# First norm of an adaLN, linear attention and SwiGLU block: the shift term of tile 1 moves to GpSimd, and the transposes of tiles 1 to 3 are reordered around the scale columns

## The chip, the cores and the metric

The kernel runs on one core of a Trainium2 chip. The metric is the device time of one execution in microseconds (us); lower is better. The profile's span (first to last instruction) is about 1.8 us shorter than the device time: the profiled run of the kernel before has a span of 827.4 us and a time of 829.23 us. Every run also reports the mean granted clock of TensorE, as a share of full speed. Six of the profiles kept, those of the kernel before and of the changed kernel among them, hold no clock records; a clock of 1.000 there means only that no slower stretch was recorded.

## The reference, cut to what matters

```python
mod = silu(c) @ w_mod                      # six rows of 1024: sa, ca, ga, sb, cb, gb
h = layernorm(x) * (1 + ca) + sa           # x: 2048 x 1024, bf16
x = x + ga * linear_attention(h, wqkv, wo) # 32 heads of 32
h = layernorm(x) * (1 + cb) + sb
x = x + gb * ((silu(h @ w_gate) * (h @ w_up)) @ w_down)
```

The change touches the first `layernorm` and the column sums that make `1 + ca`, for the first 512 rows only (tiles 0 to 3 of 128 rows). They are what stands between the start of the program and the first matmul of the q projection.

## The kernel before

The parts that matter, with cuts marked `[...]`. A helper records every operation in program order for each engine and adds the semaphore waits. An engine runs its own operations in the order written. Reads and writes of PSUM are ordered by whole banks: an engine that reads any part of a bank waits for the last TensorE operation recorded on that bank.

```python
def mod_sc(w, c0, ms):            # one column of 128 sums for each m: 8 matmuls of one column
    for m in ms:
        for kt in range(NDT):
            P.pe("matmul", out=PS[:, 0, c0 + m:c0 + m + 1], lhsT=w[:, kt, m*128:(m+1)*128], rhs=SILUC[:, kt:kt+1], [...])

def tile_transposes(*js):         # column blocks dt and dt+1 of all four tiles share a PSUM bank
    for dt in range(NDT):
        for j in js:
            P.pe("transpose", out=PSB[:, 4 + dt // 2, [...]], in_=XRES[:, j, dt*128:(dt+1)*128], identity=IDENT[:])

def act_xn(st, mean):             # shift term on VectorE, normalization on ScalarE
    P.dve("tensor_scalar", out=NMR[:, st:st+1], in0=mean, scalar1=RSTD[:, st:st+1], scalar2=-1.0, op0=ALU.mult, op1=ALU.mult)
    P.act("activation", out=XRES[:, st, :], in_=XRES[:, st, :], func=ACT.Identity, scale=RSTD[:, st:st+1], bias=NMR[:, st:st+1])

def warm(n=1, bank=2):            # matmuls that only keep TensorE's clock up
    for _ in range(n):
        P.pe("matmul", out=PS[:, bank, :], lhsT=IDENT[:], rhs=E1[:, 0, :], start=True, stop=True)

warm(13, bank=3)
[...]
act_xn(0, MV[:, 0, 0:1])
tile_transposes(0)
warm(5, bank=3)
act_var(1)                        # variance of tile 1, on VectorE
s2_[2]()                          # statistics of tile 2
P.dve("tensor_scalar", out=VE[:, 2:3], in0=MV[:, 2, 1:2], scalar1=EPS, scalar2=None, op0=ALU.add)
P.pool("tensor_tensor", out=RSTD[:, 1:3], in0=VE[:, 1:3], in1=NEGHALF[:, 0:2], op=ALU.pow)
s3_[0](); s3_[1](); s3_[2]()      # statistics of tile 3
ln1_rstd1(3)
act_xn(1, SUMX[:, 1:2])
ln1_xn(2)                         # normalization of tile 2, on VectorE
tile_transposes(2)
mod_sc(WCA, 8, range(2))          # scale columns 0-255
ln1_xn(3)
fin_ca(0, 2)
tile_transposes(1, 3)
mod_sc(WCA, 8, range(2, 4))
h0_first(0, "dve")                # first operand of q: transposed block times scale, read from PSUM
[...]
```

## Time and profile before

| | before |
|---|---|
| time, first three runs | 832.71, 833.0, 830.86 us (median 832.71) |
| profiled run | 829.23 us, span 827.4 us, granted clock 1.000 |
| TensorE busy | 816.5 us, 99% of the span |

The page's busy line of the kernel before:

```profile
PE 816.5 (99%) x4244; PEld 376.4 (45%) x4323; DVE 311.3 (38%) x665; ACT 197.4 (24%) x336; POOL 39.8 (5%) x57
```

TensorE is the limit nearly everywhere. Note also 4244 matmul records beside 4323 weight loads: 79 matmul records are missing, so a gap between two matmuls of this trace may be a missing record. Weight-load records (PEld) are complete.

The timeline of the first norm of the kernel before. Columns: start us, us, engine, line, operation, out<-in, count, and in brackets the engine's idle time before it and what ended that.

```profile
8.20 0.62 PE L176 MATMUL ps<-ident,xres 128*128 128x128 bf16 x8 [0.18 <-ACT xres L176]
8.66 1.24 PE L176 MATMUL ps<-e,ident 128*128 128x512 bf16 x5
...
8.95 0.20 DVE L176 TENSOR_SCALAR nmr<-sumx,rstd 128x1 f32<-128x1 f32 x1
...
9.24 1.24 ACT L176 ACTIVATE xres<-xres,nmr,rstd 128x1024 bf16<-128x1024 bf16 x1 [1.10 <-DVE nmr L176]
...
9.74 0.61 PE L176 MATMUL ps<-ident,xres 128*128 128x128 bf16 x8
...
10.18 0.54 PE L176 MATMUL ps<-siluc,wca 128*128 128x1 bf16 x16
...
10.59 1.05 PE L176 MATMUL ps<-ident,xres 128*128 128x128 bf16 x16
...
11.09 0.88 DVE L176 TENSOR_SCALAR ht<-ps,modcol 128x512 bf16<-128x512 bf16 x2 [0.17 <-PE ps L176]
...
11.48 0.54 PE L176 MATMUL ps<-siluc,wca 128*128 128x1 bf16 x16
...
11.86 1.20 PEld L176 LDWEIGHTS ps<-ht,wqk 128*128 128x128 bf16 x7
```

Read it as one queue on TensorE: tile 0, warm-up, tile 2, columns, tiles 1 and 3, columns, q. Each group starts where the one before it stops issuing. The `us` of a group runs to the modelled end of its last matmul, so neighbours overlap. Tile 1 is normalized from 9.24 to 10.48, because its shift term (`nmr`) waits on VectorE behind tile 3's statistics; TensorE wants it at 10.59.

### The profile page before, as it was taken

The page shows a single profiled execution, that of the slowest core. Times are in us where ns is not written, and L with a number is a line of the kernel's source. Part 1 is how long each engine was busy: PE and PEld are TensorE (multiplying, and loading weights), DVE is VectorE, ACT ScalarE, POOL GpSimd, SP SyncE. Part 2 cuts the span into 40 slices and gives each one's busy share as a digit, 9 for nine tenths or more (in the row PEclk, how much of TensorE's full clock was granted, in tenths as well). Part 3 has the DMA queues.
Part 4 walks back from the last instruction along what each step waited for, and adds up shares of the span by engine and source line. Part 5 has one row for each costly group of instructions (what it writes and reads, how often), then busy time and mean ns, then how long its engine had stood idle before and what let it go on. Part 6 is the DMA issues. An engine that isn't in the chain of part 4 may idle for free.

```text
span 827.4 us, 10429 instructions
## 1 busy us (share of the span) xinstructions
PE 816.5 (99%) x4244; PEld 376.4 (45%) x4323; DVE 311.3 (38%) x665; ACT 197.4 (24%) x336; POOL 39.8 (5%) x57
## 2 busy tenths in 40 slices
PE   8999999999999999999999999999999999999998
PEld 4544444444444444444444444444444444444444
DVE  5797987476945521121221112122111211221111
ACT  4757643123241111011111101111110111111011
POOL 1010000000130000020000003000000300000000
DMA  9969656866397985600455570045557004553000
GB/s 320 298 146 230 151 156 158 180 191 254 75 256 235 290 255 153 173 26 24 131 152 151 154 177 25 20 131 153 152 153 182 26 19 128 152 151 85 0 26 26
DMA packets 199359, 119.31 MB, mean 144 GB/s; under 512 B 57992, under 2 KB 183056, under 8 KB 199312
## 3 DMA queue, kind: packets, MB, share of 16 engines
q1 hardware_dynamic: 199296, 118.65, 53.5%
q8 instruction: 34, 0.56, 0.3%
q14 instruction: 13, 0.11, 0.0%
q10 hardware_dynamic: 16, 0.00, 0.0%
HBM read 100.67 MB, written 4.33 MB: 127 GB/s over the span
## 4 chain that ended last, share of the span: by engine, by line
PE 96%; DVE 2%; issue 1%; DMA 0%; ACT 0%; DVEq 0%; ACTq 0%
PE ps L176 96%; DVE acc L176 1%; DMA xres<-in_A_x_dram 0%; DVE stats L176 0%; DVE pkt L176 0%; DVE e L176 0%; ACT xres L176 0%; DVE pqt L176 0%; ACT e L176 0%; DVE mv L176 0%; DVE xres L176 0%; DVE ht L176 0%; DVE ve L176 0%; DVE nmr L176 0%; DVEq L247 0%
## 5 line engine op out<-in xcount | busy, mean ns | idle before, releaser
L176 PE MATMUL ps<-h2t,gug 128*128 128x512 bf16 x878 | 210.1, 379 | 0.9
L176 PE MATMUL ps<-h2t,guu 128*128 128x512 bf16 x878 | 209.9, 379 | 0.9
L176 DVE TENSOR_TENSOR at<-sg,ps 128x512 bf16<-128x512 bf16 x112 | 77.1, 688 | 282.7 <-PE ps L176 270.5
L176 ACT ACTIVATE sg<-ps 128x512 bf16<-128x512 f32 x112 | 66.9, 597 | 309.7 <-PE ps L176 298.3
L176 PEld LDWEIGHTS ps<-h2t,guu 128*128 128x128 bf16 x896 | 87.7, 98 | 105.7
L176 PEld LDWEIGHTS ps<-h2t,gug 128*128 128x128 bf16 x896 | 87.6, 98 | 105.5
L176 PE MATMUL ps<-wd_a,at 128*128 128x512 bf16 (+1 forms) x502 | 111.9, 377 | 0.5
L176 PE MATMUL ps<-ht,wqk 128*128 128x512 bf16 x499 | 110.3, 379 | 0.8
L176 PE MATMUL ps<-wd_b,at 128*128 128x512 bf16 (+1 forms) x377 | 84.6, 377 | 0.4
L176 PEld LDWEIGHTS ps<-wd_a,at 128*128 128x128 bf16 x512 | 50.1, 98 | 59.7
L176 DVE TENSOR_TENSOR ut<-att,gb_b 128x512 bf16<-128x512 bf16 (+1 forms) x32 | 14.1, 442 | 167.0 <-ACT att L176 167.0
L176 PEld LDWEIGHTS ps<-ht,wqk 128*128 128x128 bf16 x512 | 49.5, 98 | 58.7 <-DVE ht L176 0.2
L176 ACT ACTIVATE att<-ps 128x512 bf16<-128x512 f32 (+1 forms) x32 | 17.4, 591 | 182.1 <-PE ps L176 182.1
L176 PEld LDWEIGHTS ps<-wd_b,at 128*128 128x128 bf16 x384 | 37.6, 98 | 44.7
L176 PE MATMUL ps<-mw,pqt 128*128 128x512 bf16 x249 | 55.6, 379 | 1.5 <-issue 1.2
L176 PE MATMUL ps<-pk,xres 128*128 128x512 bf16 x250 | 55.4, 379 | 0.6 <-issue 0.5
L176 POOL TENSOR_SCALAR h2t<-h2t,modcol 128x512 bf16<-128x512 bf16 x32 | 26.4, 842 | 383.3 <-DMA h2t<-xn 383.3
L176 ACT ACTIVATE e<-ps 128x512 bf16<-128x512 f32 x56 | 33.2, 604 | 31.7 <-PE ps L176 19.4
L176 PEld LDWEIGHTS ps<-mw,pqt 128*128 128x128 bf16 x256 | 24.7, 98 | 31.3 <-issue 1.8
L176 PEld LDWEIGHTS ps<-pk,xres 128*128 128x128 bf16 x256 | 24.7, 98 | 29.9 <-issue 0.9
L176 ACT ACTIVATE junk<-xres 128x1024 bf16<-128x1024 bf16 x24 | 25.4, 1058 | 35.6 <-DVE xres L176 35.3
L176 DVE SCALAR_TENSOR_TENSOR xres<-ps,xres 128x512 bf16<-128x512 f32 x32 | 21.5, 688 | 12.9 <-PE ps L176 12.8
(107 smaller groups left out, 337.3 us busy)
## 6 DMA issues: line engine op xcount, KB each, us to landing
gug<-in_B_w_gate_dram SPq DMA_DIRECT2D x56, 512.0 KB, 4.0
guu<-in_B_w_up_dram SPq DMA_DIRECT2D x56, 512.0 KB, 5.3
xres<-in_A_x_dram SPq DMA_DIRECT2D x20, 256.0 KB, 7.8
rb<-recip_den SPq DMA_DIRECT2D x8, 512.0 KB, 12.1
stgx<-in_w_mod_dram SPq DMA_DIRECT2D x2, 2048.0 KB, 8.5
wd_a<-in_B_w_down_dram SPq DMA_DIRECT2D x4, 1024.0 KB, 7.6
out_dram<-xres SPq DMA_DIRECT2D x31, 128.0 KB, 1.7
xres<-in_A_x_dram SPq DMA_DIRECT2D x3, 1024.0 KB, 14.0
```

Of the source, the lines that this page charges most:

```text
L176: return getattr(e, method)(**kw)
```

## The change

The intent: tile 1's shift term no longer waits on VectorE behind tile 3, so tile 1 is normalized about a microsecond earlier; TensorE fills the time until tiles 1 and 2 are there with the first scale columns instead of tile 2; tile 3, which is ready last, is transposed last.

```diff
         act_var(1)
+        P.pool("tensor_tensor", out=RSTD[:, 1:2], in0=VE[:, 1:2], in1=NEGHALF[:, 0:1], op=ALU.pow)
+        P.pool("tensor_scalar", out=NMR[:, 1:2], in0=SUMX[:, 1:2], scalar1=RSTD[:, 1:2], scalar2=-1.0,
+               op0=ALU.mult, op1=ALU.mult)
+        P.act("activation", out=XRES[:, 1, :], in_=XRES[:, 1, :], func=ACT.Identity, scale=RSTD[:, 1:2],
+              bias=NMR[:, 1:2])
         s2_[2]()
-        P.dve("tensor_scalar", out=VE[:, 2:3], in0=MV[:, 2, 1:2], scalar1=EPS, scalar2=None, op0=ALU.add)
-        P.pool("tensor_tensor", out=RSTD[:, 1:3], in0=VE[:, 1:3], in1=NEGHALF[:, 0:2], op=ALU.pow)
+        ln1_rstd1(2)
         s3_[0]()
         s3_[1]()
         s3_[2]()
         ln1_rstd1(3)
-        act_xn(1, SUMX[:, 1:2])
         ln1_xn(2)
-        tile_transposes(2)
         mod_sc(WCA, 8, range(2))
+        tile_transposes(1, 2)
         ln1_xn(3)
         fin_ca(0, 2)
-        tile_transposes(1, 3)
+        tile_transposes(3)
         mod_sc(WCA, 8, range(2, 4))
```

## The prediction

> **What bounds the kernel.** TensorE. The page gives it 99% of the 827.4 us span, the chain of waits 96%. The change touches only the first norm (7 to 12.5 us). Narrow timelines show TensorE without a gap from 8.20 us:
>
> - tile 0's transposes from 8.20
> - five warm-ups from 8.66, the last at 9.52 (the next may start near 9.73)
> - tile 2 at 9.74
> - 16 scale columns at 10.18
> - tiles 1 and 3 at 10.59
> - 16 scale columns at 11.48
> - q's first weight load at 11.86. Its first matmul record is missing (19 beside 20 weight loads); I take it as 11.88, not the chain's 12.10.
>
> A transpose takes 55 ns of TensorE (8 in 0.44 us), a column matmul 26 ns (16 in 0.41 us). The Trainium skill, "TensorE: Matmul & The Clock Gate", section "Wait — 56ns, not 53.3ns?", gives 55.6 ns and a floor near 25 ns; the trace agrees.
>
> **What changes.** TensorE's work stays the same (24 transposes, 32 columns); only the order changes. VectorE loses one 0.20 us instruction. On GpSimd the 1x2 power (0.71 us) becomes two of 0.56 us. Powers cost 0.56, 0.71 and 1.01 us at 1, 2 and 4 elements per partition, about 0.42 us fixed: I estimate 0.4 us for the shift term. The page "GPSIMD Engine Reference", section "2.1 Instruction dispatch", speaks of about 6 us at the first call of a freshly loaded kernel; here the first GpSimd tensor-scalar (228.61 us) starts 0.1 us after its data landed, so I expect none.
>
> **Expected times.** ve of tile 1 is ready at 7.09, its power ends near 7.7, shift term near 8.2; ScalarE, free at 8.15, normalizes tile 1 from about 8.3 to 9.5 (before: 9.24 to 10.48). Tile 2 is done near 9.5, tile 3 near 10.3. TensorE: columns 0-255 at 9.73, tiles 1 and 2 at 10.15, tile 3 at 11.03, columns at 11.48, q due at 11.88. So all three tiles arrive with 0.6 us of slack; before, tile 1 had 0.1 us.
>
> **On the critical path: nothing to gain.** Before, only 0.01 us was lost at 9.74. Two things get tighter:
>
> 1. The first scaled operand (ht, dt 0) reads a PSUM bank complete only after tile 3's second transpose, now at 11.09 (before: 10.76). VectorE starts 0.26 to 0.34 us later, needs 0.48 us, ends at 11.83 to 11.91 (before 11.57). q is due at 11.88: a stall of 0 to 0.1 us.
> 2. The first half of the scale weights, issued at 2.65 and 6.9 us to landing, is there at 9.55; needed at 9.73 instead of 10.18. Slack falls from 0.6 to 0.2 us.
>
> Net estimate: +0.05 us (0 to +0.2) of 827, which passes through, since TensorE has little later idle time. Runs of before scatter over 2.1 us, so timing shows no difference.
>
> **Predicted: 832.4 us, 830.4 to 833.9.** Faster by over 2%: 0.005; within 2%: 0.985; slower by over 2%: 0.01.
>
> **In the profile:** tile 1's normalization about 1 us earlier; GpSimd's shift term near 7.8 us; columns at 9.73 right behind the warm-up; tile transposes in one run of 24 from about 10.15; first scaled operand at 11.35 to 11.45; q weights at 11.86 to 12.0; everything after shifted by that, under 0.2 us.
>
> **What would prove me wrong:** a hidden GpSimd start-up (TensorE idle for several us before tile 1); late scale weights; or gaps that missing records hid before (up to 0.3 us gained).

## More of the kernel before

Much later, between the linear attention and its output projection, TensorE gets two bursts of small matmuls (`kvt_mm`, 128 matmuls of 32 columns each).

```python
def kvt_mm(half):
    for h in range(4):
        for dt in range(NDT):
            for g in range(4):
                c0 = 512 * half + 128 * g + 32 * h
                P.pe("matmul", out=PS[32*g:32*g+32, 6, 32*h:32*h+32], lhsT=WV[:, dt, c0:c0+32], rhs=G[:, dt, c0:c0+32], [...])
```

The chain of waits of the kernel before, in the stretch from 180 to 200 us (start us, us, what).

```profile
188.47 3.91 PE ps L176 x45
192.38 1.03 issue
193.41 1.02 PE ps L176 x4
```

For 1.03 us TensorE waits for nothing that the profile names. Between weight loads the gap is 1.41 us.

## The result, and the profile after

| | before | changed |
|---|---|---|
| median of six runs | 830.83 us (830.31 to 833.0) | 830.32 us (829.56 to 831.69) |
| ratio, 95% interval | | 0.9989 (0.9974 to 1.0005) |
| profiled run | 829.23 us, span 827.4 us | 830.08 us, span 828.3 us |

A ratio here is the mean time of one kernel's fast runs over that of the other's of the same rounds, so it is not quite the ratio of the medians quoted. The class, within 2%, was forecast right. The time was not: 830.32 lies 0.08 us below the range of 830.4 to 833.9. The six runs of before now include the three that I knew (median 832.71) and three new ones at 830.49, 830.8 and 830.31. The level that I started from had dropped by 1.9 us, with no change to the kernel.

The timeline of the first norm of the changed kernel, same columns:

```profile
7.97 0.26 POOL L176 TENSOR_SCALAR nmr<-sumx,rstd 128x1 f32<-128x1 f32 x1
...
8.32 0.62 PE L176 MATMUL ps<-ident,xres 128*128 128x128 bf16 x8 [1.37 <-ACT xres L176]
...
8.78 1.24 PE L176 MATMUL ps<-e,ident 128*128 128x512 bf16 x5
...
9.23 0.78 POOL L176 TENSOR_TENSOR rstd<-ve,neghalf 128x1 f32<-128x1 f32 x1 [0.49 <-DVE ve L176]
...
9.86 0.54 PE L176 MATMUL ps<-siluc,wca 128*128 128x1 bf16 x16
10.05 0.55 DVE L176 TENSOR_SCALAR xres<-xres,mv,rstd 128x1024 bf16<-128x1024 bf16 x1 [0.44 <-POOL rstd L176]
...
10.26 1.50 PE L176 MATMUL ps<-ident,xres 128*128 128x128 bf16 x24
...
11.55 0.88 DVE L176 TENSOR_SCALAR ht<-ps,modcol 128x512 bf16<-128x512 bf16 x2 [0.88 <-PE ps L176]
...
11.60 0.54 PE L176 MATMUL ps<-siluc,wca 128*128 128x1 bf16 x16
...
12.14 0.78 PEld L176 LDWEIGHTS ps<-ht,wqk 128*128 128x128 bf16 x5
```

Everything here is 0.12 us later from the start, because tile 0's transposes begin at 8.32 instead of 8.20. So I count from tile 0's first transpose. Then the second group of columns starts at 3.28 us in both kernels (11.48 less 8.20, 11.60 less 8.32): the new order has saved TensorE nothing up to there. But q's first weight load comes at 3.82 us instead of 3.66: the change loses 0.16 us. The first scaled operand (`ht`) starts at 3.23 us instead of 2.89. VectorE stood idle 0.88 us before it, waiting for TensorE. The bank that it reads is complete only after tile 3's second transpose.

The same stretch of the chain of waits, changed kernel:

```profile
179.95 12.75 PE ps L176 x209
192.70 1.95 issue
194.65 5.56 PE ps L176 x25
```

The nameless gap is there again, 0.9 us longer (2.32 us between weight loads). The span's difference of 0.9 us between the two profiles is about 0.12 (start) plus 0.16 (the change) plus 0.91 (this gap), and two smaller parts. Most of it lies 180 us after the last line that the change touches.

The first small part is a wait near 20 us. There TensorE takes the first weights of the shift columns (`wsa`), first in the kernel before, then in the changed one:

```profile
20.23 0.66 PEld L176 LDWEIGHTS ps<-siluc,wsa 128*128 128x128 bf16 x16
20.65 0.55 PEld L176 LDWEIGHTS ps<-siluc,wsa 128*128 128x128 bf16 x16 [0.24 <-DMA wsa<-in_w_mod_dram]
```

In the kernel before they come 8.38 us after q's first weight load. In the changed kernel they had not landed (20.61 us), and it is 8.50 us. In the fourteen profiles the distance is 8.38 us four times, and 8.48 to 9.02 us in the ten in which TensorE waits for the landing. In those the landing sets the pace: an earlier q would move nothing that follows, and a later q only by what exceeds the wait.

The second is at the end of the program. From the end of VectorE's last instruction to the end of the span it takes 2.24 or 2.25 us in all four profiles without the GpSimd part of the change, and 1.90 to 1.93 us in all ten with it. So this part of the change gains about 0.33 us, which I had not predicted. GpSimd's last semaphore instruction starts 0.41 us after the one before it without that part, 0.08 us with it; why is open.

The big difference raised two questions: does the change gain or lose, and what sets the level and its scatter?

### The profile page after: what moved, and what is told of

Read it like the earlier page. It is cut to its first block, busy times and chain, and to the rows that moved or that the text cites. A ratio compares the mean times of both kernels' runs of the same rounds, so it can differ in the third digit from the quotient of the medians.

```text
span 828.3 us, 10508 instructions
## 1 busy us (share of the span) xinstructions
PE 820.3 (99%) x4323; PEld 376.0 (45%) x4323; DVE 311.5 (38%) x664; ACT 197.3 (24%) x336; POOL 40.9 (5%) x59
## 4 chain that ended last, share of the span: by engine, by line
PE 98%; DMA 0%; issue 0%; DVE 0%; ACT 0%; SPq 0%
PE ps L176 98%; DMA xres<-in_A_x_dram 0%; DVE stats L176 0%; ACT xres L176 0%; SPq L176 0%; DVE xres L176 0%; DVE mv L176 0%; DVE nmr L176 0%
```

## The experiments

Twelve kernels ran, in three calls, each call on one chip with its own 11 runs of the kernel before. My theory: in the norm the change costs 0.16 us and gains nothing; the level that I started from was a chance draw from a scatter, which comes mostly from the gap near 192 us. The rivals: the 0.9989 is real; the level belongs to the chip; the gap is a wait for data. The diffs below are against the changed kernel unless the text says otherwise; lines that only give a helper a new argument (`width`, `dts`) are left out.

All twelve were correct. In the table, "q" is q's first weight load after tile 0's first transpose; "gap" is the longest gap between weight loads from 160 to 205 us, both from the profile.

| run | ratio to before (95%) | median us | q, us | gap, us (starts at) |
|---|---|---|---|---|
| a1_same_before | 0.9998 (0.9986 to 1.001) | 830.23 | 3.66 | 2.16 (192.8) |
| a2_same_after | 1.0008 (0.9996 to 1.002) | 830.71 | 3.82 | 1.86 (193.3) |
| a3_early_only | 1.0 (0.9988 to 1.0012) | 829.99 | 3.66 | 1.99 (192.5) |
| a4_order_only | 1.0008 (0.9996 to 1.002) | 831.27 | 4.23 | 1.74 (192.8) |
| b1_pad_after | 1.0011 (0.9998 to 1.0025) | 830.85 | 3.82 | 2.18 (168.0) |
| b2_page_after | 0.9995 (0.9982 to 1.0008) | 830.03 | 3.87 | 2.31 (192.8) |
| b3_t3_split | 1.0002 (0.9988 to 1.0016) | 830.14 | 3.66 | 1.47 (193.4) |
| b4_t3_split_pad | 1.0022 (1.0007 to 1.0036) | 832.74 | 3.74 | 2.50 (167.8) |
| c1_pad101_before | 0.998 (0.9968 to 0.9992) | 828.8 | 3.92 | 0.52, none |
| c2_pad101_after | 0.9979 (0.9965 to 0.9993) | 828.45 | 3.88 | 0.52, none |
| c3_t3_split_pad101 | 0.9974 (0.9962 to 0.9986) | 828.35 | 3.73 | 0.52, none |
| c4_split6_warm4 | 0.9973 (0.9961 to 0.9985) | 828.41 | 3.71 | 0.52, none |

### The kernel before against itself

No edit but a comment line.

> The kernel before against itself. My theory: what put the result outside my range is the level I started from. The first three runs of before (830.86 to 833.0) were high by chance, the later three (830.31 to 830.8) are the usual level. So the ratio is 1.000 with an interval of about 0.999 to 1.001, a median near 830.7, a spread of 1 to 2.5 us between single runs, and most of the spread in the profile is a gap of TensorE near 192 us (1.0 us in before, 1.95 us in the changed kernel) in which it waits for nothing named. Rival: the level is a property of the chip, so all runs of this call agree within 0.5 us and only the calls differ. In the norm: first q matmul 3.65 to 3.70 us after the first transpose of tile 0.

Measured: 0.9998, as expected. Its own 5 runs span 829.42 to 830.79, and the 11 runs of before beside it 829.74 to 831.58. So the level of before is about 830.3, and single runs differ by up to 1.8 us on one chip. The rival "all runs of one call agree within 0.5 us" falls.

### The changed kernel again

No edit but a comment line.

> The changed kernel again. My theory: no gain; TensorE loses 0.18 us in the norm (first q matmul 3.86 us after the first transpose of tile 0, against 3.68 before), so the ratio is 1.000 to 1.0004, if the scatter lets it be seen. Rival, that the 0.9989 of the first measurement is real: 0.9985 to 0.9993 again.

Measured: 1.0008 (0.9996 to 1.002), not the 0.9985 to 0.9993 of the rival. The earlier 0.9989 does not repeat. The ratio lies a little above the 1.0004 that I had allowed, but two of its six runs (832.28 and 832.23) had a granted clock of 0.998 where the others had 1.000. I come back to them. In the profile q is at 3.82 us again, the same number as in the first profile of the changed kernel; before's is 3.66 in both of its profiles.

### Half of the change: the early tile 1 alone

```diff
         ln1_xn(2)
+        tile_transposes(2)
         mod_sc(WCA, 8, range(2))
-        tile_transposes(1, 2)
         ln1_xn(3)
         fin_ca(0, 2)
-        tile_transposes(3)
+        tile_transposes(1, 3)
```

> Only the first half of the change: GpSimd forms the shift term of tile 1 and ScalarE normalizes it early, with the order on TensorE of before. My theory: tile 1 was not what TensorE waited for, so the first q matmul stays 3.65 to 3.72 us after the first transpose of tile 0, and the time stays at before's within 0.1%. Rival, that tile 1 coming at the last moment held TensorE: 0.1 to 0.3 us earlier, 3.4 to 3.6 us.

Measured: tile 1 is normalized by 1.18 us after tile 0's first transpose instead of 2.28, and q stays at 3.66. So tile 1 was not what TensorE waited for before. A wait that ends just in time is not a wait that costs.

### Half of the change: the order alone

The kernel before, with TensorE's order of the changed kernel (the same edit as in the diff of the change, without the GpSimd lines).

> Only the second half: the order on TensorE of the changed kernel, with the shift term of tile 1 on VectorE after tile 3's statistics, so tile 1 is normalized about 1 us later than in the changed kernel. My theory: TensorE reaches tiles 1 and 2 about 2.05 us after the first transpose of tile 0 but tile 1 is done only about 2.35 us after it; TensorE stands still for 0.3 us, and the first q matmul comes 4.1 to 4.25 us after the first transpose of tile 0. Rival, that the order alone gives what there is to gain: 3.6 us or less.

Measured: q at 4.23 by its weight load (its first matmul record is missing), inside the expectation; the order alone costs 0.57 us, because tiles 1 and 2 stand in TensorE's queue before tile 1 is ready (transposes at 2.34 us, tile 1 done at 2.28). The profile also showed a second wait that I had feared. The weight-load line of this run:

```profile
10.21 0.47 PEld L176 LDWEIGHTS ps<-siluc,wca 128*128 128x128 bf16 x16 [0.54 <-DMA wca<-in_w_mod_dram]
```

In this run the scale weights landed at 10.2 us, not 9.55, and held the columns for about 0.27 us (columns at 1.81 us after tile 0's first transpose, 1.54 in the changed kernel). Here tile 1 would have held TensorE anyway, but the slack of 0.2 us that I gave the weights is within what their landing varies. Together the two halves say: the GpSimd part is needed by the new order, and only by it.

### Tile 3 not quite last

```diff
-        tile_transposes(1, 2)
+        tile_transposes(1, 2, dts=range(4))
         ln1_xn(3)
         fin_ca(0, 2)
-        tile_transposes(3)
+        tile_transposes(3, dts=range(2))
+        tile_transposes(1, 2, dts=range(4, 8))
+        tile_transposes(3, dts=range(2, 8))
```

> The changed kernel, with tile 3's transposes for the first two column blocks moved ahead of the second half of tiles 1 and 2, so the first PSUM bank is complete after 10 transposes instead of 18. My theory of the 0.16 us that the change costs: the first scaled operand waits for that bank, and q for the operand. Then the first weight load of q comes 3.63 to 3.69 us after the first transpose of tile 0 (changed kernel 3.82, before 3.66), and the first scaled operand about 2.75 to 2.95 us after it (changed 3.22). Rival, that the later columns or the weights' landing hold q: still 3.8. The time can't show it: ratio 0.999 to 1.001.

Measured: the first scaled operand at 2.77 us and q at 3.66 us. The lines of this run (tile 0's first transpose is at 8.96):

```profile
11.73 0.88 DVE L176 TENSOR_SCALAR ht<-ps,modcol 128x512 bf16<-128x512 bf16 x2 [0.44 <-PE ps L176]
...
12.62 0.34 PEld L176 LDWEIGHTS ps<-ht,wqk 128*128 128x128 bf16 x3
```

The 0.16 us are back at q. (In this profile they did not last: the shift weights landed only at 21.57 us, and TensorE waited for them.) So their cause is the order of the last transposes: the first PSUM bank was complete only after 18 of the 24, here after 10.

### The gap near 192 us: 78 more instructions

The 13 warm-up matmuls of 512 columns become 52 of 128: the same columns, 39 more matmuls and 39 more weight loads ahead of everything else.

```diff
-        warm(13, bank=3)
+        warm(52, bank=3, width=128)
```

> The changed kernel with its 13 warm-up matmuls of 512 columns cut into 52 of 128 columns: the same columns, 39 more matmuls, so 78 more instructions (weight load and matmul) ahead of all that follows. My theory of the scatter: the gap of TensorE near 192 us (1.4 to 2.3 us between weight loads in six profiles) is a wait for instructions. TensorE's instructions come in 16 KB packets, 256 at a time; the packet before the gap [...] is asked for only in the burst of 256 instructions at 187 to 188 us. Moved by 78 instructions, the request falls before the burst, near 181 us: the gap near 192 falls below 0.5 us and the ratio is 0.9975 to 0.9988. Rival, that the gap is a wait for data, a PSUM bank or a reloaded x tile: gap unchanged at 1.4 to 2.3 us, ratio 0.9995 to 1.0010.

Measured: no gain (1.0011); my expectation of the time was wrong. But the gap near 192 us is gone, and a new one of the same kind stands at 168 us, in the other burst of small matmuls. The timeline of this run around it:

```profile
166.96 1.23 PE L176 MATMUL ps<-g,wv 128*32 128x32 bf16 x125
170.19 0.20 PE L176 MATMUL ps<-g,wv 128*32 128x32 bf16 x3 [2.00 <-issue]
```

TensorE stops three matmuls before the end of a burst of 128, all of them alike and with nothing new to wait for. A wait for data is hard to square with that.

The trace has the DMA queue that brings TensorE's instructions (`q8 instruction`), in packets of 16 KB. In the changed kernel's first profile one such packet runs while the gap lasts. The DMA view, window 192 to 193.2 us, has this line (packets, MB, share of 16 engines):

```profile
q8 instruction: 1, 0.02, 5.8%
```

It runs from 192.09 to 193.20 us; TensorE starts again at 194.65. The kernel's 34 packets for about 8,700 instructions of TensorE (4323 matmuls, 4323 weight loads, 70 others) are about 256 instructions each. The Trainium skill says the same in "Runtime: NRT & Kernel Launch", section "Instruction fetch mechanics": refills come "in 16 KiB blocks (256 instructions)". Here is every gap above 0.6 us from q's start on in the first ten profiles, except two near 20 us (0.86 us in a3, 0.84 us in b3), which are the wait for the shift weights, with the number of weight loads and matmuls issued before it (twice the count of weight loads):

| profile | gap starts | instructions before it | packet ends | gap ends |
|---|---|---|---|---|
| before | 192.00 | 2742 | 191.96 | 193.41 |
| changed | 192.32 | 2742 | 193.20 | 194.65 |
| a1_same_before | 192.78 | 2742 | 193.54 | 194.94 |
| a2_same_after | 193.25 | 2742 | 193.86 | 195.10 |
| a3_early_only | 192.54 | 2742 | 193.24 | 194.52 |
| a4_order_only | 192.76 | 2742 | 193.05 | 194.49 |
| b3_t3_split | 193.35 | 2742 | 193.54 | 194.82 |
| b1_pad_after (+78) | 168.01 | 2230 = 2742 - 512 | 168.80 | 170.20 |
| b4_t3_split_pad (+78) | 167.84, 193.46 | 2230, 2742 | 168.62, 192.76 | 170.34, 194.16 |
| b2_page_after (+256) | 192.79 | 2998 = 2742 + 256 | 193.47 | 195.10 |

The gap always falls at the same place of the instruction count, up to a multiple of 256, whatever the work is that stands there. And TensorE always starts again 1.2 to 1.7 us after a packet's end; what fills that time the profile does not show.

### The control: 256 more instructions

```diff
-        warm(13, bank=3)
+        warm(141, bank=3, width=48)
```

> The control: the warm-up cut into 141 matmuls of 48 columns, 128 more matmuls, so 256 more instructions: one whole packet. If the gap is a wait for instructions, moving by a whole packet puts the boundary back to the same place, and the gap near 192 us is 1.4 to 2.4 us again, ratio 0.9995 to 1.0010. If cutting the warm-up itself (clock, start) brings a gain, this one shows it too: ratio below 0.9990 with the gap still there.

Measured: the gap is back at 192.8 us with 2.31 us, the ratio 0.9995. The timeline:

```profile
192.13 1.04 PE L176 MATMUL ps<-mw,pqt 128*128 128x512 bf16 x4
195.10 1.02 PE L176 MATMUL ps<-mw,pqt 128*128 128x512 bf16 x4 [1.93 <-issue]
```

A shift by one whole packet changes nothing, and cutting the warm-up brings nothing by itself. With 78 more the gap moved, with 256 it came back: it is a wait for instructions.

### Both edits, with the badly chosen shift

Tile 3 split, and the warm-up of 52.

> Both: the split of tile 3 and the 78 more instructions in the warm-up. If both theories hold: q at 3.63 to 3.69 us after the first transpose of tile 0, no gap above 0.5 us near 192 us, ratio to before 0.9975 to 0.9988, and less scatter than before, within 1.5 us between single runs.

Measured: 1.0022, slower, with three of its five runs at a clock of 0.998; the expectation failed, as in b1. But the profiled run is one of those three, so the profile shows what the low clock is. Windows of 1 us in this run; columns: window, length, then busy us (and instructions) of PE, PEld, DVE, ACT and POOL, then the granted clock, the DMA share and GB/s:

```profile
168.00:169.00 1.00, 0.03 (x4) 0.00 (x0) 1.00 (x2) 0.00 (x0) 0.00 (x0) 1.00 1.03 209
169.00:170.00 1.00, 0.00 (x0) 0.00 (x0) 0.40 (x1) 0.00 (x0) 0.00 (x0) 1.00 0.64 127
170.00:171.00 1.00, 0.33 (x4) 0.34 (x5) 0.40 (x2) 0.00 (x0) 0.00 (x0) 0.55 0.06 16
171.00:172.00 1.00, 1.00 (x3) 0.34 (x3) 1.00 (x2) 0.00 (x0) 0.00 (x0) 0.50 0.06 16
172.00:173.00 1.00, 1.00 (x3) 0.30 (x2) 0.68 (x2) 0.00 (x0) 0.00 (x0) 0.50 0.00 0
173.00:174.00 1.00, 1.00 (x5) 0.47 (x4) 0.00 (x0) 0.00 (x0) 0.00 (x0) 0.74 0.73 90
```

The granted clock falls to half at 170.10 us, 2.26 us into the gap of 2.50 us, and stays there for 3.413 us (to 173.51 in the trace). I estimate that about half of that, 1.6 to 1.7 us, is lost on top of the gap. This is the clock gate that the Trainium skill describes in "TensorE: Matmul & The Clock Gate", section "What's actually happening", with its window of 3413 ns; the length agrees to the nanosecond that the trace gives. The mean clock of such a run is 0.998. 11 runs of this or other kernels took 832 us or more with a reported clock, and all 11 had a clock of 0.998; no run at 1.000 took more than 831.93. Among the 38 runs of before in the three calls these are 3 (832.21, 832.28, 832.34); the other 35 lie between 829.3 and 831.58. That the 832.71 and 833.0 of the first three runs were such runs is likely from this, but not shown: their clock was not reported.

### A better shift: 202 more instructions, on both kernels

```diff
-        warm(13, bank=3)
+        warm(114, bank=3, width=58)
```

> The kernel before with its 13 warm-up matmuls cut into 114 of 58 columns: 101 more matmuls, 202 more instructions. The 78 more instructions moved the gap from 192 us into the burst at 168 us (2.2 and 2.5 us there), and 256 put it back to 192 us (2.3 us), so it is a wait for instructions and the shift was badly chosen. With 202 more, each burst of 256 small matmul instructions (166.6 to 167.8 and 187.1 to 188.5 us) is cut about in half by a packet's boundary, and at least 5 us of long matmuls lie between a request and its boundary. Theory: no gap above 0.6 us at 165 to 200 us, ratio 0.9972 to 0.9988, and no run with a granted clock of 0.998. Rival, that some wait of 1 to 2 us always turns up here: ratio 0.9992 or more.

> The same in the changed kernel. Theory: the same gain, ratio to before 0.9974 to 0.9990, and no run at clock 0.998. With the scatter of the instruction wait gone, the changed kernel should stand 0.16 us (0.0002) behind the kernel before with the same 202 instructions; q's first weight load 3.82 us after the first transpose of tile 0 in this one, 3.66 in the other.

Measured: 0.998 and 0.9979, inside what was expected, and no gap: the longest time between weight loads from 160 to 205 us is 0.52 us, an ordinary one. The same lines as above in the second of them:

```profile
191.61 0.43 PE L176 MATMUL ps<-wo,kvt 32*32 32x512 bf16 x16
191.98 4.71 PE L176 MATMUL ps<-mw,pqt 128*128 128x512 bf16 x21
```

The medians fall from 830.52 (11 runs of before) to 828.8 and 828.45, by 1.7 and 2.1 us: about the length of the gap. Two points missed. One of c2's six runs had a clock of 0.998 (830.94 us); it was not the profiled one, so where its clock fell is open. And q did not come at 3.66 in c1, but at 3.92, for a reason of its own:

```profile
12.22 0.76 PEld L176 LDWEIGHTS ps<-ht,wqk 128*128 128x128 bf16 x5 [0.17 <-DMA wqk<-in_A_wqkv_dram]
```

In that run the weights of q landed at 12.2 us, 9.1 us after their issue (8.4 in a1). The same landing, at 12.30 us, set q's 3.87 in b2. So the 0.16 us between the two orders did not show between c1 and c2, and it can't show in times at all.

### The version with everything

Tile 3 split and 202 more instructions; then also four warm-ups after tile 0 instead of five, with tile 3's first two transposes after 12 others.

> The changed kernel with tile 3 split and 202 more instructions. Theory: q's first weight load 3.63 to 3.69 us after the first transpose of tile 0, no gap above 0.6 us at 165 to 200 us, ratio 0.9972 to 0.9988.

> As the one before, with four warm-up matmuls after tile 0 in place of five and tile 3's first two transposes after 12 instead of 8 of the others, so the columns start 0.22 us earlier. This is the version in which the early tile 1 should at last be worth something. Theory: columns 1.33 us after the first transpose of tile 0, q's first weight load 3.42 to 3.55 us after it, if the scale weights have landed by then; ratio 0.9970 to 0.9986. Rival, that the weights are not there yet: the columns still come at 1.45 us or later.

Measured: 0.9974 and 0.9973, both inside. c3's five runs lie within 0.4 us (828.12 to 828.5), but c1's within 1.4, c4's within 1.0 and c2's, without the one at 0.998, within 1.1 us; the 35 runs of before at 1.000 lie within 2.3 us. So the level fell; that the scatter came mostly from the gap, as my theory had it, is not shown. c3's q at 3.73 is 0.04 outside, because the scale weights were late:

```profile
10.17 0.47 PEld L176 LDWEIGHTS ps<-siluc,wca 128*128 128x128 bf16 x16 [0.39 <-DMA wca<-in_w_mod_dram]
```

The columns came 1.59 us after tile 0's first transpose (at 8.58) instead of 1.54, and the tile transposes at 2.01 instead of 1.94. c4 shows why a still earlier start is not to be had: its columns started at 1.44 us instead of the 1.33 expected, because the scale weights had landed only at 9.88 us (issue at 2.65, 7.2 us to landing), and its q at 3.71 us (12.19), because q's weights had landed only at 12.15. The rival was right. Early in the program the loads set the pace once TensorE is ready. c3 beats the kernel before by 0.26% (the changed kernel did not run beside it). Most of that comes from the instruction wait, for c1, which changes nothing else, already has 0.20%; 0.33 us, or 0.04%, is the shorter end. The norm gives next to nothing.

## Why the prediction was right or wrong

- **The step that failed: the level.** The predicted 832.4 took before's level from the three runs known then (median 832.71), as far as the recorded text shows, and its range was drawn around that. The level is about 830.4: 830.35, 830.53 and 830.52 are the medians of 11 runs in three calls. The base term was 2 us too high, so the range missed by 0.08 us. That it missed at all was the draw: the second six runs of the changed kernel (a2) have a median of 830.71, inside the range. The evidence was at hand: the profiled run of before took 829.23, and two of the three runs stood 2 us above the third. I named the scatter (2.1 us) but did not ask what it was. The runs showed four parts:
  - an instruction wait, 1.4 to 2.3 us long, in every profile of the two kernels;
  - in some runs a mean clock of 0.998, which in the one such run that was profiled was a half clock for 3.4 us;
  - the start: tile 0's first transpose came at 8.20 to 9.30 us, in all fourteen profiles 2.83 or 2.84 us after the third load of x had landed;
  - the landing of the shift weights, which held TensorE for up to 0.64 us.

  With the start of the shift columns, the instruction wait (the gap less an ordinary 0.22 us) and the end of the program taken off the span, twelve of the fourteen profiles leave the same 803.6 to 803.8 us; b4 leaves about 1.8 us more (most of it the half clock) and b1 0.6 us more (cause not found).
- **"On the critical path: nothing to gain": right.** The second group of columns starts 3.28 us after tile 0's first transpose in both kernels, and the early tile 1 alone leaves q at 3.66. What the change gained lies elsewhere, 0.33 us at the end of the program.
- **The stall of 0 to 0.1 us at q: right in kind, too small.** It is 0.16 us, twice measured, and goes away when the bank is complete earlier. VectorE started at the late end of my interval (11.55, expected 11.47 to 11.57 with the 0.12 us later start); TensorE then took another 0.1 us after VectorE's end, which I had not added. The net of +0.05 (0 to +0.2) holds it. That it "passes through" failed where the shift weights were late.
- **"Slack falls from 0.6 to 0.2 us" for the scale weights: right, and thin.** In the changed kernel's two profiles the columns came at 1.54 us, unheld; in five others that use the new order (a4, b4, c2, c3, c4) the weights were late.
- **The shift term: 0.26 us, estimated 0.4.** No start-up of several microseconds on GpSimd came: this tensor-scalar started 0.11 us after the power before it had ended. "GPSIMD Engine Reference", section "2.1 Instruction dispatch", gives its 6 us for the first call of a freshly loaded kernel; whether this call is one, no run here shows. One thing I did not foresee: tile 3's power took 0.78 us instead of 0.56, so VectorE waited 0.44 us for it and tile 3 was done at 2.27 us after tile 0's first transpose, not about 2.1. TensorE wants it at 2.8, so it costs nothing. Why it took longer stays open.
- **"TensorE has little later idle time": incomplete.** True in sum, but the gap near 192 us is the largest thing to be won, and the wait for the shift weights decides whether a shift at q is passed on.

Whether the change gains or loses in time is not settled by times: 0.9989 and 1.0008, both with 1 in their intervals. By the profiles it loses 0.16 us at q, which is passed on only where the shift weights are there in time, and gains 0.33 us at the end: together 0.02 to 0.04% faster, far below the scatter.

## What to carry to other kernels

Before predicting a time, ask what the scatter of the old kernel is made of, and centre on the profiled run and all others, not on a median of three. A tile that arrives just in time costs nothing, and making it earlier gains nothing unless what follows in TensorE's queue, and the loads it needs, can move up too; look also at which PSUM bank the next reader waits for. In a long unrolled program, a gap of TensorE that the chain calls "issue" after a burst of many small matmuls may be a wait for instructions: move the burst against the 256-instruction boundaries, for instance by cutting warm-up matmuls finer, and check that the gap does not turn up elsewhere.

## What the Trainium skill lacked or had wrong

- "Runtime: NRT & Kernel Launch", section "Instruction fetch mechanics", says that crossing a 16 KiB boundary is "mostly hidden". Here one crossing left a gap of 1.4 to 2.5 us in each of ten profiles, after a burst in which 256 instructions were used up in 1.2 us. The DMA engines were busy then (share about 1.05 near 190 us), but as busy in c2, which has no gap; whether a quieter DMA would help was not tested. TensorE started again 1.2 to 1.7 us after the packet's end. The page does not warn of bursts of small matmuls, nor name the remedy (ratio 0.998 with 202 more instructions).
- "TensorE: Matmul & The Clock Gate", section "What's actually happening", puts the fall to half clock after at least one idle window of about 3.4 us. In b4 it came 2.26 us into a gap of 2.50 us between weight loads, with a burst of matmuls on 32 columns before it; what counts as idle for the window no run here shows. The half-clock stretch itself, 3.413 us, agrees with the page.
